# Second product of the last pair of blocks in seven products for eight, with its result turned by VectorE and stored in runs of 128 bytes

## The chip, the core and the metric

The kernel runs on one core of a Trainium2 chip. The metric is the device time in microseconds (us) of one execution, as a median over runs; the runs of one kernel lie within a few us of each other. Engines are named as the profile names them: PE is TensorE's matmul, PEld its weight load (beside PE), DVE is VectorE, ACT is ScalarE, POOL is GpSimd, SP is SyncE, which issues most DMAs; SPq and ACTq are DMA issues by SP and ACT. Each engine runs its own instructions strictly in order and waits at an instruction until what it needs is there.

## The reference, cut to what matters

A linear attention over 8 batches, 8 heads, 576 positions and head size 64 gives a matrix `x` of 4608 tokens by 512 columns. A feed-forward follows, and it is nearly all of the TensorE work:

```
h = x @ w_in          # (4608, 512) @ (512, 2048)
r = maximum(h, 0)
g = r * r
return g @ w_out      # (4608, 2048) @ (2048, 512)
```

All is float32. Each float32 operand of a matmul is split in a high and a low part, and a product is three matmuls: high by high, high by low, low by high. One part is made by a cast on ACT, the other by a subtraction on DVE or POOL.

## The kernel before, in words

The tokens are worked off in 9 blocks of 512. Blocks 0 to 2 go one by one. Blocks 3 to 8 go as three **pairs** of 1,024 tokens, called `s0`, `s1`, `s2` in the order. For a pair the first product `h` is already made with seven block products for eight (`A11 S4 S2 A12 S3 S1 A22`), for each of 8 column groups j: the weights and their sums are the stationary operand, and DVE and ACT put the products together on the two 512-token halves, the near and the far one.

The second product of a pair is made plainly. `out_unit(s, n, t)`, in the order `s1.o.n.t`, is three matmuls: 128 tokens of `g` as the stationary operand, one 128-row chunk of `w_out` (512 columns) moving. There are 32 chunks n (0 to 15 near half, 16 to 31 far half) and 4 row tiles t, so 384 matmuls for a pair. The chunks of the near half are spread through the j loop; those of the far half come behind it, as the stretch `o.16` to `o.31`. In the profile the moving operand of these matmuls is called `wp`, `wo` or `wo_back`, by where the chunk lies (a refilled ring tile, or one that was kept: of the far half `wo_back` are the chunks 17, 19, 24 and 28, `wo` 21, 26 and 30).

The `g` of the far half is made just ahead of its use. `hf` is a cast on ACT (`g<-far`), `lf` a subtraction on DVE (`g<-far,g`), two of each for a pair of chunks. Only two `g` tiles exist, each for two chunks, so `hf` and `lf` of the chunks 24 and 25 can't begin before PE is through with chunk 21, and PE needs them at chunk 24.

In the same stretch of `s1`, the operands for the first product of `s2` are made: sums `T`, their high parts (`xh_T`, ACT) and their low parts (`xl_T`, `xl_B`: DVE, some on POOL). In the order they are `x2.T*`, `x2.h*`, `x2.l*` and `x2.p*` (p is POOL).

A result is copied from PSUM (`ev`, the tile `o`, by ACT and DVE in turn) and stored in rows of 512 columns (`st`, `out_dram<-o`). SP also refills a ring of seven tiles (`refill`, `wp<-...`) with weights from DRAM.

The order of all this is a table of names written out by hand, `LIST`: the kernel emits the units in that order, and each engine gets its instructions in it. All instructions are recorded by one helper, so the profile shows them under the helper's line (L290 before, L309 after); tiles tell them apart.

Of the kernel before, what the change touches and what calls it, by code (L numbers as in the profile page):

```python
# [8 lines left out]
F32 = mybir.dt.float32  # L9
# [39 lines left out]
X_BANK, Y_BANK, Z_BANK = 1, 3, 7  # L49

# [48 lines left out]
h22_0 c0/2.1 glo21 h22_1 Lq/3.2 kx/2.3 d0/2.1 h22_2 qs/3.0 P1/2.1 h22_3 c1/2.1 o.20.0 w7.WA d1/2.1 qy/3.0 relu22
o.20.1 qm/3.1 rm22 P2/2.1 o.20.2 tb/3.0 c2/2.1 XL/2.1 xh0/2.1 o.20.3 d2/2.1 Bw/3.0 xl0/2.1 qm/3.2 h23_0 ghi22 qd/3.1  # L100
P3/2.1 glo22 h23_1 c3/2.1 qh0/2.2 h23_2 d3/2.1 Lq/3.3 w0.a1 kv/2.2 xh1/2.1 qh1/2.2 xl1/2.1 ql0/2.2 h23_3 qx/3.1
Lv/3.1 kr/2.2 o.21.0 relu23 qs/3.1 ql1/2.2 o.21.1 rm23 o.21.2 kh/2.2 qm/3.3 o.21.3 kp/2.2 B/2.3 kp/2.3 w0.s2 h24_0
ghi23 w0.s3 h24_1 glo23 h24_2 w0.s4 Lk/3.0 h24_3 kl/2.2 w0.h34 o.22.0 w0.l34 Lk/3.1 relu24 P0/2.2 o.22.1 rm24 w1.a1
o.22.2 c0/2.2 Lv/3.0 qy/3.1 w0.h12 d0/2.2 o.22.3 P1/2.2 w0.l12 ghi24 h25_0 km/3.0 c1/2.2 h25_1 h25_2 w0.W34 glo24
h25_3 d1/2.2 w0.W12 km/3.1 o.23.0 relu25 P2/2.2 XL/2.2 o.23.1 rm25 k1/3.0 o.23.2 c2/2.2 xh0/2.2 o.23.3 xl0/2.2
d2/2.2 h26_0 k2/3.0 ghi25 w1.a2 P3/2.2 h26_1 c3/2.2 glo25 qh0/2.3 h26_2 w1.s1 d3/2.2 h26_3 ql0/2.3 k1/3.1 xh1/2.2
o.24.0 relu26 o.24.1 rm26 ke/3.0 P0/2.3 o.24.2 c0/2.3 xl1/2.2 o.24.3 qh1/2.3 d0/2.3 k2/3.1 h27_0 ql1/2.3 ghi26 h27_1
kx/3.0 glo26 h27_2 w1.s2 B/3.0 P1/2.3 h27_3 ke/3.1 c1/2.3 o.25.0 relu27 d1/2.3 w1.s3 o.25.1 tb/3.1 rm27 XL/2.3 w1.s4
P2/2.3 o.25.2 c2/2.3 Bw/3.1 qd/3.2 xh0/2.3 o.25.3 d2/2.3 P3/2.3 ghi27 h28_0 xl0/2.3 Lq/4.0 c3/2.3 glo27 h28_1 kx/3.1
kz/3.0 d3/2.3 h28_2 w2.a1 xh1/2.3 kv/3.0 qh0/3.0 xl1/2.3 qx/3.2 ql0/3.0 h28_3 Lv/3.2 w1.h34 kr/3.0 o.26.0 relu28  # L110
qs/3.2 kp/3.0 o.26.1 kp/3.1 rm28 o.26.2 kh/3.0 qm/4.0 qy/3.2 o.26.3 w1.h12 Lk/3.2 h29_0 ghi28 kl/3.0 h29_1 w1.l12
glo28 Lk/3.3 P0/3.0 tb/3.2 h29_2 c0/3.0 Lv/3.3 w1.l34 h29_3 qd/3.3 P1/3.0 relu29 o.27.0 km/3.2 rm29 o.27.1 c1/3.0
o.27.2 qx/3.3 B/3.1 k1/3.2 o.27.3 h30_0 ghi29 k2/3.2 h30_1 XR/3.0 Lq/4.1 h30_2 glo29 h30_3 km/3.3 o.28.0 Bw/3.2
relu30 w1.W34 o.28.1 rm30 ke/3.2 o.28.2 qh0/3.1 w1.W12 k1/3.3 o.28.3 kx/3.2 ql0/3.1 XL/3.0 h31_0 ghi30 k2/3.3 h31_1
h31_2 B/3.2 w2.a2 glo30 P0/3.1 qs/3.3 h31_3 c0/3.1 w2.s1 o.29.0 relu31 XL/3.1 P1/3.1 ke/3.3 rm31 o.29.1 back.0
# [33 lines left out]
s0.0.m21 s0.R.9 s0.o.0.2 d0/5.0 s0.0.h1 Lq/6.0 s0.o.0.3 qx/5.2 s0.0.l1 P1/5.0 s0.1.A11 qs/5.2 s0.R.10 c1/5.0 st.2.3
d1/5.0 s0.0.S4 qy/5.2 s0.1.c1 k2/5.2 XL/5.0 P2/5.0 s0.o.1.0 s0.R.11 c2/5.0 s0.0.a12 s0.1.S2 d2/5.0 s0.0.rf0 tb/5.2  # L150
P3/5.0 s0.1.A12 s0.1.u2 k1/5.3 qd/5.3 Bw/5.2 c3/5.0 s0.o.1.1 d3/5.0 s0.R.12 qx/5.3 XR/5.0 s0.1.S3 s0.1.r11 qs/5.3
Lq/6.1 s0.1.S1 s0.1.m11 qy/5.3 s0.1.u3 qm/6.0 s0.1.h0 s0.o.1.2 s0.R.13 s0.0.qf0 s0.1.l0 s0.o.1.3 s0.1.a22 s0.1.A22
# [157 lines left out]
def attention_ffn_kernel(ctx: ExitStack, tc: tile.TileContext, q, k, v, w_in, w_out, out):  # L310
# [820 lines left out]
    X, Y, Z = (banks[i] for i in (X_BANK, Y_BANK, Z_BANK))  # L1131
    g_tiles = {}

    def g_at(s, n):
# [202 lines left out]
```

## Time and profile before

| | |
|---|---|
| median of 3 runs | 840.65 us (838.52 to 841.83) |
| profiled execution | 838.89 us |
| its span in the profile | 837.1 us |
| PE busy | 828.8 us, 99% |
| DVE busy | 540.8 us, 65% |
| ACT busy | 486.7 us, 58% |
| POOL busy | 288.2 us, 34% |

The span runs from the first to the last instruction or DMA of the profiled execution; 1.8 us of its time lie around it. Busy shares are means over stages: DVE's 65% is made of stretches in which it is nearly full and others in which it is nearly idle.

### The profile page before, as it was taken

How to read it: one execution, taken by the hardware profiler on the slowest of the kernel's cores; microseconds unless marked ns; L12 is line 12 of the kernel's file. 1: busy time of each engine (PE TensorE's matmuls, PEld its weight loads, DVE VectorE, ACT ScalarE, POOL GpSimd, SP SyncE). 2: the span in 40 equal slices, each digit the busy share in tenths (PEclk: the TensorE clock that was granted, in tenths of full speed). 3: DMA queues.
4: the chain of work that ended last, by engine and by line, in shares of the span. 5: the costliest groups of instructions: out<-in, count | busy, mean ns of one | idle time of the engine just before them, and what ended most of it. 6: DMA issues, size and time to landing. Idle time of an engine off the chain costs nothing.

```text
span 837.1 us, 12969 instructions
## 1 busy us (share of the span) xinstructions
PE 828.8 (99%) x4286; PEld 678.2 (81%) x4286; DVE 540.8 (65%) x1098; ACT 486.7 (58%) x898; POOL 288.2 (34%) x269
## 2 busy tenths in 40 slices
PE   8999999999999999999999999999999999999997
PEld 6778787888888888888888888888888888888886
DVE  7898888878787789957687887653257132222421
ACT  4888866666656656676667455566464144444411
POOL 4578654467667656242322342211004000000000
PEclk9999999999999999999999999999999999999999
DMA  9969987973688889999889857865575375554611
GB/s 240 270 186 299 279 287 214 327 215 98 211 256 249 227 283 259 277 281 258 234 252 245 283 159 213 271 187 189 172 233 177 98 227 156 163 166 154 186 55 50
DMA packets 156594, 179.65 MB, mean 215 GB/s; under 512 B 51696, under 2 KB 120304, under 8 KB 156528
## 3 DMA queue, kind: packets, MB, share of 16 engines
q1 hardware_dynamic: 155776, 177.88, 71.7%
q10 hardware_dynamic: 752, 0.95, 0.4%
q8 instruction: 34, 0.56, 0.3%
q14 instruction: 32, 0.26, 0.1%
HBM read 133.69 MB, written 45.09 MB: 214 GB/s over the span
## 4 chain that ended last, share of the span: by engine, by line
PE 90%; DVE 4%; DMA 2%; issue 1%; POOL 1%; ACT 1%; SPq 1%; DVEq 0%; POOLq 0%; ACTq 0%
PE bank L290 90%; DVE m L290 1%; DMA raw_o<-in_moe_w_out_dram 1%; DMA qt<-in_q_dram 1%; SPq L290 1%; DMA raw_i<-in_moe_w_in_dram 0%; POOL qs L290 0%; DVE qs L290 0%; DVE g_lo L290 0%; DVE w L290 0%; POOL qn L290 0%; DVE xf L290 0%; DVE bank L290 0%; DVE r L290 0%; DVE qm L290 0%
## 5 line engine op out<-in xcount | busy, mean ns | idle before, releaser
L290 PE MATMUL bank<-wp,g 128*128 128x512 f32 x648 | 160.7, 390 | 0.0
L290 PEld LDWEIGHTS bank<-wp,g 128*128 128x128 f32 x648 | 120.6, 188 | 24.9
L290 PE MATMUL bank<-x_hi,wi 128*128 128x512 f32 x384 | 131.3, 396 | 0.0
L290 PE MATMUL bank<-xh_T,wp 128*128 128x512 f32 x384 | 130.7, 390 | 0.0
L290 PE MATMUL bank<-wo,g_hi 128*128 128x512 f32 x384 | 120.3, 394 | 0.0
L290 PE MATMUL bank<-xh_B,wp 128*128 128x512 f32 x288 | 98.0, 390 | 0.0
L290 POOL TENSOR_TENSOR qs<-qT,qs 64x640 fp32r<-64x640 f32 (+1 forms) x40 | 64.2, 1604 | 94.4 <-ACT qs L290 63.1
L290 DVE TENSOR_TENSOR c<-c,bank 128x512 f32<-128x512 f32 x48 | 32.9, 686 | 86.7 <-ACT c L290 86.4
L290 PEld LDWEIGHTS bank<-xh_T,wp 128*128 128x128 f32 x384 | 72.1, 188 | 16.3 <-ACT bank L290 1.2
L290 PEld LDWEIGHTS bank<-x_hi,wi 128*128 128x128 f32 x384 | 72.2, 188 | 15.9 <-DVE x_lo L290 0.4
L290 ACT ACTIVATE far<-far 128x512 f32<-128x512 f32 x96 | 60.6, 632 | 41.1 <-DVE far L290 39.9
L290 PEld LDWEIGHTS bank<-wo,g_hi 128*128 128x128 f32 x384 | 70.5, 188 | 14.8 <-ACT g_hi L290 0.4
L290 PE MATMUL bank<-wo,g_lo 128*128 128x512 f32 x192 | 75.0, 391 | 0.0
L290 PE MATMUL bank<-x_lo,wi 128*128 128x512 f32 x192 | 74.9, 390 | 0.0
L290 PE MATMUL bank<-xl_T,wp 128*128 128x512 f32 x192 | 74.8, 389 | 0.0
L290 PE MATMUL bank<-wo_back,g 128*128 128x512 f32 x288 | 71.4, 389 | 0.0
L290 DVE TENSOR_TENSOR g<-far,g 128x512 fp32r<-128x512 f32 x48 | 35.7, 781 | 43.5 <-ACT g L290 43.4
L290 DVE TENSOR_TENSOR far<-far,bank 128x512 f32<-128x512 f32 x48 | 32.9, 685 | 47.7 <-PE bank L290 47.5
L290 PEld LDWEIGHTS bank<-xh_B,wp 128*128 128x128 f32 x288 | 54.1, 188 | 11.6
L290 PEld LDWEIGHTS bank<-wo_back,g 128*128 128x128 f32 x288 | 53.6, 188 | 11.0
L290 POOL TENSOR_TENSOR qn<-qn,qs 128x640 f32<-128x640 f32 x30 | 37.8, 1261 | 69.6 <-DVE qs L290 47.0
L290 ACT CAST g<-far 128x512 fp32r<-128x512 f32 x48 | 27.5, 619 | 49.7 <-PE bank L290 49.4
(136 smaller groups left out, 1527.0 us busy)
## 6 DMA issues: line engine op xcount, KB each, us to landing
wp<-w_outs SPq DMA_DIRECT2D x54, 512.0 KB, 4.4
wp<-w_sums SPq DMA_DIRECT2D x96, 256.0 KB, 3.8
wp<-w_own SPq DMA_DIRECT2D x72, 256.0 KB, 3.6
out_dram<-o SPq DMA_DIRECT2D x68, 128.0 KB, 2.9
raw_i<-in_moe_w_in_dram SPq DMA_DIRECT2D x16, 512.0 KB, 6.5
raw_o<-in_moe_w_out_dram SPq DMA_DIRECT2D x16, 512.0 KB, 7.1
bounce<-tb SPq DMA_DIRECT2D x24, 320.0 KB, 3.8
qT<-bounce SPq DMA_DIRECT2D x96, 80.0 KB, 2.8
```

Of the source, the lines that this page charges most:

```text
L290: ins = f(*args, **kwargs)
```

## The change

Only the last pair, `s2`, gets another second product. It is made with seven block products for eight as well: `w_out` (or sums of its quarters) becomes the stationary operand and `g` (or sums of its quarters) the moving one, 512 tokens wide. A product has 8 j by 2 column tiles d by 3 matmuls, 48 in all, and seven of them are 336 matmuls in place of 384.

- **Sums of `w_out`** (`out_sums(j)`, `t0` to `t7`, recorded in `s1`): for each j DVE makes two sums of 128x512 (`a1`, `a2`), two differences of 128x256 (`s3`, `s4`) and one low part of 128x512 (`l34`); POOL makes two differences of 128x256 (`s1`, `s2`) and one low part of 128x512 (`l12`); ACT makes two casts (`h12`, `h34`); SP stores the four halves to a new DRAM tensor `w_t`. The buffers are those of the attention, which is over by then: in the rows below they appear as `qt`, `kt`, `vt` and `sum_*`.
- **In the j loop of `s2`**: no `o` chunks; `fp.A11.j` and `fp.A12.j` (6 matmuls each) and four sums of `g` on DVE (`q.S1` to `q.S4`). The refills are those of a new list (`refill_last`), 56 tiles in place of 46.
- **Behind it**: `fp.S2`, `S1`, `S4`, `S3`, `A22`, each from casts on ACT (`fh`) and subtractions on DVE or POOL (`fl`), tile `fo`.
- **The result**: for each of C11, C12, C22, C21 and each column half d, DVE adds from PSUM (`fe`, into `o`, or into `p`, `u` on the way), turns the tile by 32x32 blocks (`ft`, `STREAM_TRANSPOSE turned<-o`), and SP or ACT stores it in runs of 32 columns (`fs`): four DMAs of 16 KB in each `fs` of C11 and C12, two of 32 KB in each of C21 and C22.

```diff
+LAST_ORDER = "A11 S2 A12 S3 S1 A22 S4".split()
+FINAL = ("S2", "S1", "S4", "S3", "A22")
+FINAL_BANKS = dict(S2=(1, 3), S1=(0, 7), S4=(2, 6), S3=(4, 5), A22=(1, 3))
...
+    def out_sums(j):
...
+        return dict(
+            a1=lambda: add(a1, 2 * j), a2=lambda: add(a2, 2 * j + 1),
+            s1=less(e.pool, s_, 0, a1, 1, a1, 0), s2=less(e.pool, s_, 1, a2, 1, s_, 0),
+            s3=less(e.dve, a2, 1, a2, 1, a1, 1), s4=less(e.dve, a2, 0, a2, 0, s_, 1),
+            h12=high(0), l12=low(0, e.pool), W12=lambda: save(0),
+            h34=high(1), l34=low(1, e.dve), W34=lambda: save(1),
+        )
...
+    def last_sum(name, j, on):
...
+        on.tensor_tensor(out, a, b, op=op)
...
+    def final_product(p, j, ds):
...
+        for d in ds:
+            f = slice(d * P, (d + 1) * P)
+            for k, (a, b) in enumerate(((0, 0), (0, 1), (1, 0))):
+                e.pe.matmul(
+                    banks[to[d]], w[:, a, f], x[:, b], start=j == 0 and k == 0, stop=j == NPR - 1 and k == 2,
+                    skip_group_check=True,
+                )
...
+    def final_out(name, d):
...
+        e.dve.tensor_tensor(out, base, bank(p), op=ALU.add)
+
+    def final_turn(name, d):
+        t = evac["t" + name, d] = w_pool.tile([P, NT], F32, name="turned", tag="w", bufs=WB)
+        e.dve.transpose(
...
+    def final_store(name, d, a, on):
...
+        for b in range(2):
...
+                on.dma_start(dst[:, :, b], src[:, :, b])
...
+fp.A22.4.1 fs.C22.1.3.a fp.A22.5.1 fs.C22.0.0.s fp.A22.6.1 fs.C22.0.2.s fp.A22.7.1 fe.C21.1 fs.C22.1.0.s ft.C21.0
+fs.C21.0.1.a fs.C21.0.0.s fs.C21.0.3.a ft.C21.1 fs.C21.0.2.s fs.C21.1.1.a fs.C21.1.0.s fs.C21.1.3.a fs.C21.1.2.s
+fs.C22.1.2.s
```

DVE before, in `s1` from the low parts for the chunks 20 and 21 to those of the last chunks; each `g<-far,g x2` is the `lf` of two chunks, the rest are operands for `s2`:

```order
L290 TENSOR_TENSOR g<-far,g 128x512 x2
L290 TENSOR_TENSOR T_6879<-xl_T_3480,xl_B_3061 128x512
L290 TENSOR_TENSOR xl_B_3061<-xl_B_3061,xh_B_3175 128x512
L290 TENSOR_TENSOR T_6891<-xl_B_3717,xl_T_3480 128x512
L290 TENSOR_TENSOR xl_T_3769<-T_6879,xh_T_3764 128x512
L290 TENSOR_TENSOR g<-far,g 128x512 x2
L290 TENSOR_TENSOR T_6921<-xl_B_3717,T_6879 128x512
L290 TENSOR_TENSOR T_6929<-xl_B_3371,T_6921 128x512
L290 TENSOR_TENSOR xl_T_3813<-T_6921,xh_T_3803 128x512
L290 TENSOR_TENSOR xl_T_3480<-T_6891,xh_T_3798 128x512
L290 TENSOR_TENSOR g<-far,g 128x512 x8
```

DVE now, from the low parts for the chunks 22 and 23 (the sixth row above) on; `qt`, `kt`, `vt` and `sum_*` hold the sums of `w_out`:

```order
L309 TENSOR_TENSOR g<-far,g 128x512 x2
L309 TENSOR_TENSOR T_6996<-xl_B_3718,T_6940 128x512
L309 TENSOR_TENSOR qt_80<-wo_957 128x512
L309 TENSOR_TENSOR T_7007<-xl_B_3372,T_6996 128x512
L309 TENSOR_TENSOR xl_T_3814<-T_6996,xh_T_3804 128x512
L309 TENSOR_TENSOR xl_T_3481<-T_6959,xh_T_3799 128x512
L309 TENSOR_TENSOR qt_80<-qt_80,kt_78 128x256
L309 TENSOR_TENSOR qt_80<-qt_80,vt_86 128x256
L309 TENSOR_TENSOR kt_79<-wp 128x512
L309 TENSOR_TENSOR qt_80<-qt_80,sum_qn 128x512
L309 TENSOR_TENSOR g<-far,g 128x512 x2
L309 TENSOR_TENSOR qt_81<-wp 128x512
```

Five instructions of the sums now stand between two pairs of low parts that had four between them, and the same goes on behind the last row, where before nothing stood between the low parts.

DVE at the very end of the program, now; `p` and `u` are partial sums, bank_89 and bank_91 hold the last product A22 for the two column halves of C21:

```order
L309 TENSOR_TENSOR o<-u_8232,bank_93 128x512
L309 TENSOR_TENSOR p_8006<-p_8006,bank_92 128x512
L309 STREAM_TRANSPOSE turned<-o 128x512
L309 TENSOR_TENSOR p_8018<-p_8018,bank_93 128x512
L309 TENSOR_TENSOR o<-p_8006,bank_89 128x512
L309 STREAM_TRANSPOSE turned<-o 128x512
L309 TENSOR_TENSOR o<-p_8018,bank_91 128x512
L309 STREAM_TRANSPOSE turned<-o 128x512 x2
```

Where two copies out of PSUM ended the program before, the add that needs the last matmul now stands ahead of the turns of both halves of C21.

SP at the very end, now, with the waits: `DMAHW` is one of eight completion counters that SP's and ACT's DMAs take in turn, `DVE` is DVE's:

```order
L309 DMA out_dram<-turned 32x8x32 [waits DMAHW1_49,DVE_49]
L309 DMA out_dram<-turned 32x8x32 [waits DMAHW3_49]
L309 DMA out_dram<-turned 32x8x32 [waits DMAHW5_49]
L309 DMA out_dram<-turned 32x8x32 [waits DMAHW7_49]
L309 DMA out_dram<-turned 32x8x32 [waits DMAHW1_49,DVE_49]
L309 DMA out_dram<-turned 32x8x32 [waits DMAHW3_49]
L309 DMA out_dram<-turned 32x8x32 [waits DMAHW4_49]
L309 DMA out_dram<-turned 32x8x32 [waits DMAHW5_49]
L309 DMA out_dram<-turned 32x8x32 [waits DMAHW6_49]
L309 DMA out_dram<-turned 32x8x32 [waits DMAHW7_49]
```

Ten stores stand behind the turn of C21's first half on SP (the first four of them its own), and ACT has eight more of the same form; each waits for the completion of the DMA that last used its counter.

## Rows read from the trace of the kernel before

**Rows 1.** The profile's page: busy us (share of the span) and instructions of each engine.

```profile
PE 828.8 (99%) x4286; PEld 678.2 (81%) x4286; DVE 540.8 (65%) x1098; ACT 486.7 (58%) x898; POOL 288.2 (34%) x269
```

**Rows 2.** The chain that ended last: start us, us, what; its end.

```profile
194.58 637.71 PE bank L290 x3178
832.28 0.02 issue
832.31 0.69 DVE o L290
```

**Rows 3.** Stretches of s1 (first two) and of one round of s2's j loop.

```profile
core 0: us, PE busy (x) PEld busy (x) DVE busy (x) ACT busy (x) POOL busy (x), PEclk, DMA share, GB/s
618.31:644.15 25.84, 25.84 (x115) 21.40 (x114) 22.06 (x31) 16.09 (x28) 7.78 (x5) 1.00 0.66 209
644.15:655.03 10.88, 10.88 (x49) 9.01 (x48) 3.77 (x5) 2.28 (x4) 2.33 (x2) 1.00 0.45 143
682.79:697.75 14.96, 14.96 (x68) 12.39 (x67) 4.13 (x7) 6.71 (x11) 0.00 (x0) 1.00 0.58 174
```

**Rows 4.** Timeline of PE: start us, us, instructions; one chunk of s1, and the end.

```profile
646.87 2.88 PE L290 MATMUL bank<-wo_back,g 128*128 128x512 f32 x12
...
826.67 2.88 PE L290 MATMUL bank<-wo,g 128*128 128x512 f32 x12
829.39 2.88 PE L290 MATMUL bank<-wp,g 128*128 128x512 f32 x12
```

**Rows 5.** Timeline of DVE from 638 us: the same, with idle time before and its releaser.

```profile
638.16 1.41 DVE L290 TENSOR_TENSOR T<-xl_B,T 128x512 f32<-128x512 f32 x2
639.53 2.39 DVE L290 TENSOR_TENSOR xl_T<-T,xh_T 128x512 fp32r<-128x512 f32 x2
642.34 2.98 DVE L290 TENSOR_TENSOR g<-far,g 128x512 fp32r<-128x512 f32 x2 [0.42 <-ACT g L290]
647.78 1.30 DVE L290 TENSOR_TENSOR g<-far,g 128x512 fp32r<-128x512 f32 x2 [2.46 <-ACT g L290]
```

**Rows 6.** Timeline of POOL in the same stretch.

```profile
639.65 1.72 POOL L290 TENSOR_TENSOR xl_B<-xl_B,xh_B 128x512 fp32r<-128x512 f32 x1 [6.39 <-DVE T L290]
641.33 1.74 POOL L290 TENSOR_TENSOR xl_T<-T,xh_T 128x512 fp32r<-128x512 f32 x1
643.04 3.43 POOL L290 TENSOR_TENSOR xl_B<-xl_B,xh_B 128x512 fp32r<-128x512 f32 x2
```

**Rows 7.** Groups of DVE by form: count | busy us, mean ns of one | idle before.

```profile
L290 DVE TENSOR_TENSOR c<-c,bank 128x512 f32<-128x512 f32 x48 | 32.9, 686 | 86.7 <-ACT c L290 86.4
...
L290 DVE STREAM_TRANSPOSE tb<-qn 128x640 f32<-128x640 f32 x24 | 20.1, 838 | 3.8 <-POOL qn L290 2.6 <-DMA out_dram<-o 1.0
...
L290 DVE TENSOR_TENSOR xr<-bank,xf 64x256 f32<-64x256 f32 x48 | 19.7, 411 | 10.7 <-ACT xf L290 10.2
...
L290 DVE TENSOR_TENSOR a<-wi 128x512 f32<-128x512 f32 x8 | 8.0, 1005 | 1.5 <-POOL a L290 1.4
```

**Rows 8.** Groups of POOL by form.

```profile
L290 POOL TENSOR_TENSOR s<-s,w_sum 128x512 fp32r<-128x512 f32 x8 | 10.4, 1295 | 6.2 <-ACT w_sum L290 6.2
...
L290 POOL TENSOR_TENSOR s<-a 128x256 f32<-128x256 f32 x8 | 6.4, 795 | 6.0 <-DVE mt L290 3.1 <-DMA w_sums<-s 2.6
```

**Rows 9.** Group of ACT by form.

```profile
L290 ACT CAST g<-far 128x512 fp32r<-128x512 f32 x48 | 27.5, 619 | 49.7 <-PE bank L290 49.4
```

**Rows 10.** Timeline of DMA issues by SP: eight stores of results in a row.

```profile
787.36 5.01 SPq L290 DMA_DIRECT2D out_dram<-o  x8
```

**Rows 11.** The page's DMA issues: xcount, KB each, median us from issue to landing.

```profile
out_dram<-o SPq DMA_DIRECT2D x68, 128.0 KB, 2.9
...
x_left<-xf SPq DMA_DIRECT2D x16, 32.0 KB, 3.4
```

**Rows 12.** One store of `x_left` (32 KB, runs of 128 bytes): issue ns, landing us.

```profile
L290 SPq DMA_DIRECT2D x_left<-xf x1: 371/371/371, 434.8 to 434.8; - x1
DMA to landing us min/median/max: 2.1/2.1/2.1
```

More of the change, by code (lines that the diff above doesn't have):

```diff
@@ L99 @@
[L99 to L103, printed above, removed]
@@ L149 @@
[L149 to L152, printed above, removed]
-tb/5.3 s0.1.rf1 ke/5.2 s0.o.2.0 s0.1.r21 B/5.1 s0.o.2.1 qd/6.0 kx/5.2 s0.1.m21 s0.o.2.2 k2/5.3 s0.1.h1 s0.o.2.3
@@ L1129, in product @@
                 )
-    X, Y, Z = (banks[i] for i in (X_BANK, Y_BANK, Z_BANK))
+    Y, Z = (banks[i] for i in (Y_BANK, Z_BANK))
+    last_c = {}
     g_tiles = {}
@@ L1141, in wide @@
         c = {}
+        X = banks[X_OTHER if s == LAST and j % 2 else X_BANK]
+        if s == LAST:
+            last_c[j] = c
         def near(i):
@@ L1193, in wide @@
         return u
+    w_t = dram.tile([NPR, 2, P, 2, 2, 2 * P], F32, name="w_t")
+    seq = [(j, p) for j in range(NPR) for p in LAST_ORDER]
+    last_tiles = []
+    for n in range(0, len(seq), 2):
+        last_tiles.append(("w", seq[n : n + 2]))
+        if n % 7 in (5, 6):
+            j = len([1 for t in last_tiles if t[0] == "b"])
+            last_tiles.append(("b", j))
+    for p in FINAL:
+        last_tiles += [("f", (p, i)) for i in range(NPR // 2)]
+    final_w, final_op, slots, evac = {}, {}, {}, {}
@@ new lines, in refill_last @@
+    def refill_last(n):
+        kind, i = last_tiles[n]
+        t = stay.tile([P, 2, 2, 2 * P], F32R, name="wp", tag=RING[(LAST * len(tiles_of) + n) % len(RING)])
+        for k in range(2):
+            if kind == "w":
+                j, name = i[k]
+                held[LAST, (j, name)] = t[:, k]
+                if name[0] == "A":
+                    src = w_own[j, :, ("A11", "A12", "A22").index(name)]
+                else:
+                    a, m = divmod(int(name[1]) - 1, 2)
+                    src = w_sums[j, a, :, :, m]
+            elif kind == "b":
+                src = w_outs[2 * i + k][:, :, : 2 * P]
+                final_w[("A11", "A12")[k], i] = t[:, k]
+            else:
+                j = 2 * i[1] + k
+                final_w[i[0], j] = t[:, k]
+                name = FINAL_OF[i[0]]
+                if name == "B22":
+                    src = w_outs[2 * j + 1][:, :, 2 * P :]
+                else:
+                    a, m = {"T1": (0, 0), "T2": (0, 1), "T4": (1, 0), "T3": (1, 1)}[name]
+                    src = w_t[j, a, :, :, m]
+            e.sp.dma_start(t[:, k].bitcast(F32), src)
@@ new lines, in spare, with buffer, add, less @@
+    def spare(n):
+        if n not in spares:
+            if n < 7:
+                t = (kt[0], kt[1], qt[0], qt[1], vt[0], vt[1], qT)[n].rearrange("p a b c -> p (a b c)")
+            else:
+                name = ("q_lo", "q_hi", "qn", "ke")[n - 7]
+                t = attn_pool.tile([P, 2 * LOW * D], F32, name="sum_" + name, tag=name)
+            spares[n] = t[:, :NT]
+        return spares[n]
+    spares = {}
+    def out_sums(j):
+        def buffer(n):
+            return spare(n).rearrange("p (c f) -> p c f", c=2)
+        i = j % 2
+        a1, a2, s_ = (lambda: buffer(i)), (lambda: buffer(2 + i)), (lambda: buffer(4 + i))
+        hi = (lambda: buffer(7 + i)), (lambda: buffer(9 + i))
+        low_of = s_, a2
+        def add(t, fc):
+            w = wo_at[fc] if fc in wo_at else wo_at[LAST - 1, fc + NFC * (j < SUMS_LATE)]
+            e.dve.tensor_tensor(
+                t().rearrange("p c f -> p (c f)"), w[:, 0].bitcast(F32), w[:, 1].bitcast(F32), op=ALU.add
+            )
+        def less(on, out, k, a, ka, b, kb):
+            return lambda: on.tensor_tensor(out()[:, k], a()[:, ka], b()[:, kb], op=ALU.subtract)
+        def high(n):
+            return lambda: e.act.copy(hi[n]().bitcast(F32R), low_of[n]())
+        def low(n, on):
+            t = low_of[n]
+            return lambda: on.tensor_tensor(t().bitcast(F32R), t(), hi[n](), op=ALU.subtract)
+        def save(n):
+            e.sp.dma_start(w_t[j, n, :, 0], hi[n]())
+            e.sp.dma_start(w_t[j, n, :, 1], low_of[n]())
+        return dict(
[5 more added lines that the diff above has]
+        )
@@ new lines, in slot @@
+    def slot(n):
+        if n not in slots:
+            if n < 11:
+                slots[n] = spare(n)
+            elif n < 17:
+                t = stay.tile([P, 2, NT], F32, name="sum", tag=f"o{KEPT[(n - 11) // 2]}")
+                slots[n], slots[n + 1] = t[:, 0], t[:, 1]
+            else:
+                t = late.tile([P, 4, NT], F32, name="sum", tag="x_hi1" if n == 17 else "x_lo1")
+                for i in range(4):
+                    slots[n + i] = t[:, i]
+        return slots[n]
@@ new lines, in last_source @@
+    def last_source(name, j):
+        c = last_c[j]
+        if name in ("S3", "A22"):
+            return c["far"][:, name == "A22"]
+        return slot(3 * j + ("S1", "S2", "S4").index(name))
+    def last_sum(name, j, on):
+        c = last_c[j]
+        out = last_source(name, j)
+        a, b, op = dict(
+            S1=(c["far"][:, 0], c["far"][:, 1], ALU.add), S2=(last_source("S1", j), c[0], ALU.subtract),
+            S3=(c[0], c["far"][:, 0], ALU.subtract), S4=(c[1], last_source("S2", j), ALU.subtract),
+        )[name]
+        on.tensor_tensor(out, a, b, op=op)
@@ new lines, in final_out, with bank, fresh @@
+    def final_out(name, d):
+        def bank(p):
+            return banks[{"A11": (2, 6), "A12": (4, 5)}.get(p, FINAL_BANKS.get(p))[d]]
+        def fresh():
+            evac[name, d] = w_pool.tile([P, NT], F32, name="o", tag="raw", bufs=RAWB)
+            return evac[name, d]
+        if name == "p1":
+            evac["p1", d] = work.tile([P, NT], F32, name="p1", tag=f"r{d}")
+            return e.act.copy(evac["p1", d], bank("A11"))
+        p1 = evac["p1", d]
+        if name == "U4":
+            evac["U4", d] = work.tile([P, NT], F32, name="u4", tag=f"g_hi{d}")
+        base, p = dict(
+            C11=("p1", "A12"), U2=("p1", "S2"), U4=("p1", "S1"), C12=("U4", "S4"),
+            C22=("U4", "S3"), U3=("p1", "S3"), C21=("p1", "A22"),
+        )[name]
+        base = evac[base, d] if name != "U4" else p1
+        out = fresh() if name[0] == "C" else evac["U4", d] if name == "U4" else p1
+        e.dve.tensor_tensor(out, base, bank(p), op=ALU.add)
@@ L1284, in run @@
             elif args[0] == "R":
-                refill(s, int(args[1]))
+                if s == LAST:
+                    refill_last(int(args[1]))
+                else:
+                    refill(s, int(args[1]))
             else:
```

386 lines of the change are left out of this document (230 added, 156 removed).

## The prediction

> **What bounds the kernel now.** I read the page first: PE is busy for 99% of the span, all other engines well below [rows 1]. Then the chain of waits: from 194.58 us on it is PE alone for 637.71 us, 3178 matmuls without one wait in it, up to the last matmul's end at 832.28; behind that stand one copy on DVE and the stores [rows 2]. So any matmul that is taken away shortens the run by its own length, as long as nothing makes PE wait, and all that is put behind the last matmul is added. The table of stretches then shows what has room beside PE, at a granted clock of 1.00 throughout [rows 3]. In the far half's chunks of s1 it is little on DVE: from chunk 14 to chunk 23 (618.31 to 644.15) it is busy for 22.06 of 25.84 us. In s2's j loop there is much: 4.13 of 14.96 us for DVE, 6.71 for ACT.
>
> **The matmuls.** Twelve matmuls start 829.39 - 826.67 = 2.72 us after the twelve before [rows 4], 0.2267 us each. 336 in place of 384 are 48 fewer: **-10.9 us**. Before, stationary and moving operands were 128x128 and 128x512 too, and weight loads lay beside the matmuls, so the size of one matmul stays as it is.
>
> **The sums of w_out, beside PE.** By the order they begin at chunk 10 of s1. In the j loop a set of them is 3 x 0.69 + 2 x 0.41 = 2.9 us of DVE, some 4 with what POOL costs it (below), beside 4 us that the loop takes in 15: room enough, 0 taken (0 to 1). From chunk 14 to 23, though, stand nine sums, four low parts (13 x 0.69 us, by c<-c,bank) and eight differences (0.41 us, by the 256-wide xr<-bank,xf) [rows 7]: 8.9 + 3.3 = 12.2 us. With 22.06 that is 34.3 us in 25.84, over by 8.5.
>
> POOL's part makes it worse. The two xl_T and the two low parts on DVE took 2.39 and 2.98 us, beside POOL's own subtractions; without a neighbour such pairs took 1.41 and 1.30 [rows 5, 6]. POOL was busy there for 1.72 + 1.74 + 3.43 = 6.89 us, and DVE lost 1.0 + 1.7 = 2.7, so 0.39 us for each us of POOL. POOL gets eight differences of 0.795 and four low parts of 1.295 in this stretch [rows 8], 11.5 us: 4.5 us more on DVE, 13.0 us over in all.
>
> Who waits for it: DVE works in order, and the low parts of the far half's g stand among the sums. Those for chunk 24 were done at 642.34 + 2.98 = 645.32 [rows 5]; PE begins that chunk at 646.87 [rows 4]. So 1.55 us of lateness are free; what is beyond makes PE wait, at the chunks 20, 22, 24, each time some us. With 13.0 over, 11.4 us reach PE; without any effect of POOL it would be 6.9; and if the new work also spread POOL's work so that the 2.7 us lost before were not lost again, 4.2. From chunk 23 to 27 five full-size and four half-size instructions of the sums (5.1 us) and some 3 us by POOL join 3.77 us of 10.88 [rows 3]: no catching up, no more loss. I take **+10 us** (4 to 18; the upper end is the third rival), nearer to 11.4 than to 6.9 because rows of this very stretch show DVE lengthened.
>
> Here a rule bears on it: the Trainium skill, "SBUF — State Buffer", section "SBUF: two separate sides", says that a DVE instruction with two SBUF inputs and a GpSimd one that reads SBUF exclude each other for a whole instruction. The trace doesn't show that fully: the two low parts ended at 645.32 while POOL was busy to 646.47 [rows 5, 6].
>
> **s2's j loop.** A round has 54 matmuls, 12.24 us, in place of 66. Beside it DVE has 4.13 + 4 x 0.69 = 6.9 us, ACT its 6.71 [rows 3, 7]. Both fit, POOL is idle: 0. Nor do the products behind the loop wait: one lasts 10.9 us and needs eight casts of 0.62 [rows 9] and about six subtractions of 0.69, and all adds and turns put together leave DVE under 9.6 us for each. The refills have seven tiles of lead and land in under 5 us before: 0.
>
> **Behind the last matmul.** Before, 837.1 - 832.28 = 4.8 us [rows 2]: a copy, a store, its landing. Now: the last add (0.69, by c<-c,bank), then the turn of C21's first half, which stands behind it by the order (838 ns for 640 columns, 0.67 for 512), so 1.4 us until the first stores of C21 can be issued [rows 7]. SP then has ten stores to issue, at 5.01 / 8 = 0.63 us each [rows 10]; the last begins at 1.4 + 9 x 0.63 = 7.1 us. Landing takes 2.9 to 3.4 us [rows 11], and a few tenths end the span: 10.5 to 11, **+6 us**. The low bound: 0.37 us for an issue and 2.1 for a landing, as the one x_left store of the same shape took in a quiet stretch [rows 12], 1.4 + 3.3 + 2.1 = 6.8, so +2. The high bound: each store waits for the one eight before it, so 18 stores are three turns of 3.4 us or more behind 1.4, and SP may come late from the stores before: 14, so +9. I stay near the rows of out_dram, since these are the same queue at the same place.
>
> On this the Trainium skill ("DMA: Bandwidth & Descriptors", section "Specifications") asks for 512 bytes or more in a run. In the rows, 32 KB in runs of 128 bytes took 3.4 us to land, 128 KB in runs of 2 KB 2.9 [rows 11]: the rule points to the upper half of that term; no run yet shows its size for 18 stores together.
>
> **Sum.** -10.9 + 10 + 6 = +5.1 us. On the profiled execution (838.89) that is 844.0, on the median of the runs (840.65), 1.8 us higher, 845.7. I forecast **845 us**.
>
> **Rivals.**
> 1. *DVE is hardly late (faster).* Place: the low parts for the chunks 20 to 28. If DVE's idle time of before chunk 14 lets the sums run ahead, or the half-size differences take far less than 0.41 us, lateness stays near the 1.55 us of slack, and PE waits 0 to 2 us. Then -10.9 + 1 + 5 = -4.9, **835.5**. It decides from some 7 us less DVE work than I count. For it: the mean share of DVE is only 65% [rows 1]. Against: 34.3 us in 25.84 without any help of POOL. Chance 0.14.
> 2. *A smaller lateness and a short tail.* 5 us of waits, and 4 behind the last matmul: -2, **838.5**. For it: the sum without POOL, and the x_left store. Chance 0.24.
> 3. *POOL blocks DVE for its whole time.* All 11.5 us of POOL count: 22.06 + 12.2 + 11.5 - 25.84 - 1.55 = 18.4 us of waits, -10.9 + 18.4 + 6 = +13.5, **854**. It is what the exclusion would do here. Against: 0.39, not 1, in the rows. Chance 0.08.
> 4. *The stores are the larger cost.* Waits of 10 us, and a tail of 14: +8, **849**. Chance 0.14.
>
> **Numbers.** My forecast (842 to 848) has 0.40. No change that the measurement of this kernel can tell is 0.5%, 4.2 us: 836.4 to 844.9. Rival 1 is nearly all of faster: 0.13. Rival 2 and the lower part of mine (845 lies on the border, so 0.12 of the 0.40) are within: 0.36. The rest is slower: 0.51. The range for 8 in 10 is **836 to 852**: it leaves out most of the first rival's lower side and of the third.
>
> **What would show it.** In the profile after: 48 matmuls fewer in s2 and rounds of 12.24 us; PE waits released by DVE (tile g) at the chunks 20, 22, 24, 26 and 28 of s1, about 10 us in sum, with DVE busy nearly without gap from about 618 us and POOL busy beside it; low parts of 1.0 to 1.7 us each there; no wait of PE in s2; 10.5 to 11 us from the last matmul to the end, filled by SP's issues. The prediction is wrong if PE's chain stays unbroken in s1 (then DVE's sums were hidden), if waits appear in s2's loop or products instead, or if the end lasts under 7 or over 14 us.

## The result and the profile after

The changed kernel takes 851.91 us (850.5 to 853.36), against 840.78 before: the ratio is 1.0136, with a 95% interval of 1.0108 to 1.0164. The forecast was 845 us. It had the direction and the two places right. The time lies just inside the range for 8 in 10 (836 to 852) and outside that of the forecast itself (842 to 848): of the change forecast from 840.65 to 845 us, 4.4 us, the run shows 11.1.

The profiled execution took 852.65 us, its span (from its first to its last instruction) is 850.8. The page: busy time of each engine.

```profile
PE 824.2 (97%) x4238; PEld 670.2 (79%) x4238; DVE 615.9 (72%) x1202; ACT 505.5 (59%) x936; POOL 327.0 (38%) x303
```

PE has 48 matmuls fewer than in [rows 1] and DVE 75 us more to do. PE was one unbroken chain before [rows 2]; now it waits. The view of waits of PE from 560 us on: who was waited for, us in all, times, longest.

```profile
PE bank L309 <- DVE g L309: 5.3, 4, 1.7
PE bank L309 <- ACT g L309: 2.6, 3, 1.8
PE bank L309 <- DVE o L309: 0.6, 1, 0.6
```

All of it lies in the far half's chunks of s1: 0.6 us at chunk 16 (for a copy out of PSUM, tile o), 3.3 at chunk 22, 1.9 at 24, 1.7 at 26 and 1.0 at 28, and none over 0.3 us at 20. The timeline of PE there, which answers to [rows 4]:

```profile
619.13 2.88 PE L309 MATMUL bank<-wo,g 128*128 128x512 f32 x12
...
648.29 6.75 PE L309 MATMUL bank<-wp,g 128*128 128x512 f32 x22 [1.51 <-DVE g L309]
655.42 0.73 PE L309 MATMUL bank<-wo_back,g 128*128 128x512 f32 x2 [0.38 <-ACT g L309]
657.63 4.06 PE L309 MATMUL bank<-wo_back,g 128*128 128x512 f32 x10 [1.48 <-DVE g L309]
...
678.81 1.52 PE L309 MATMUL bank<-wo,g 128*128 128x512 f32 x6
```

Chunk 14 starts at 619.13, which was 618.31 [rows 3]: 0.8 us were lost before. Most of it is lost at one wait of 0.3 us for POOL's qs at 463.5 us, where the order of the work is the same in both kernels, so this isn't the change's. Chunk 24 starts at 655.42 in place of 646.87, 7.7 us later than that shift explains. Chunk 30 would be six times 2.72 us behind chunk 24 in the kernel before, at 663.19; it starts at 678.81, **14.8 us** late beside the shift. The table of stretches shows the two reasons (columns as in [rows 3]).

```profile
641.40:648.00 6.60, 3.56 (x15) 2.31 (x13) 6.52 (x7) 2.80 (x5) 4.92 (x4) 1.00 0.56 197
648.00:651.40 3.40, 3.11 (x7) 2.48 (x8) 3.40 (x6) 1.34 (x3) 1.22 (x2) 0.51 0.97 354
651.40:658.20 6.80, 4.95 (x20) 3.45 (x19) 6.67 (x9) 2.15 (x4) 4.26 (x3) 0.99 0.36 108
658.20:661.60 3.40, 3.40 (x10) 2.62 (x9) 2.49 (x3) 0.62 (x1) 2.68 (x3) 0.52 1.02 314
```

DVE (third pair of numbers) is busy for 19.1 of these 20.2 us. And the granted clock (the number behind POOL's) is at 0.51 and 0.52 in two stretches of 3.4 us, the lower of TensorE's two levels (1.2 in place of 2.4 GHz); ahead of each, PE had been busy for only 3.56 of 6.60 and 4.95 of 6.80 us.

PE's waits for ACT are 2.6 us of the 8.5. ACT works in order too, and its casts of g stand there behind casts of the sums, which wait for DVE. ACT's timeline ahead of chunk 22:

```profile
644.85 0.62 ACT L309 CAST sum_ke<-qt 128x512 fp32r<-128x512 f32 x1 [1.24 <-DVE qt L309]
645.38 1.13 ACT L309 CAST g<-far 128x512 fp32r<-128x512 f32 x2
```

In s2 nothing waits. The six matmuls of one of the two products made in its loop start 12.24 us apart (three rows of PE's timeline), as the prediction worked out:

```profile
703.56 1.52 PE L309 MATMUL bank<-g,wp 128*128 128x512 f32 x6
...
715.80 1.52 PE L309 MATMUL bank<-g,wp 128*128 128x512 f32 x6
...
728.04 1.52 PE L309 MATMUL bank<-g,wp 128*128 128x512 f32 x6
```

The end, from the timelines of PE, SP, ACT and DVE:

```profile
819.61 17.39 PE L309 MATMUL bank<-fo,wp 128*128 128x512 f32 x76
822.56 26.21 SPq L309 DMA_DIRECT2D out_dram<-turned  x40
828.13 18.62 ACTq L309 DMA_DIRECT2D out_dram<-turned  x24
832.25 0.71 DVE L309 STREAM_TRANSPOSE turned<-o 128x512 f32<-128x512 f32 x1 [1.57 <-DMA out_dram<-turned]
837.16 0.71 DVE L309 STREAM_TRANSPOSE turned<-o 128x512 f32<-128x512 f32 x1 [3.04 <-DMA out_dram<-turned]
837.01 11.76 SPq L309 DMA_DIRECT2D out_dram<-turned  x22
837.91 8.84 ACTq L309 DMA_DIRECT2D out_dram<-turned  x12
842.09 0.71 DVE L309 STREAM_TRANSPOSE turned<-o 128x512 f32<-128x512 f32 x1 [3.64 <-DMA out_dram<-turned]
844.15 0.71 DVE L309 STREAM_TRANSPOSE turned<-o 128x512 f32<-128x512 f32 x1 [1.35 <-DMA out_dram<-turned]
```

The last matmul ends at 819.61 + 17.39 = 837.00, and 13.8 us follow (4.8 before). At that moment 22 stores are still to be issued on SP and 12 on ACT (the parts of their rows from 837 us on). SP issues 40 stores in a row from 822.56 on, 0.66 us each on the mean, which includes some 4 us of waits for DMAs that refill tiles, as SP's view of waits from 815 us on has it:

```profile
SPq L309 <- DMA wp<-w_t: 4.0, 3, 2.0
```

The turns wait for DMAs, since a turned tile's buffer (there are three) is free only when its stores have landed.

From chunk 30 to the last matmul it was 832.28 - 663.19 = 169.1 us, and is 837.0 - 678.81 = 158.2. So the account of the profiled spans closes: +0.8 (before chunk 14) + 14.8 (s1) - 10.9 (matmuls) + 9.0 (end) = +13.7 us, and 850.8 - 837.1 is 13.7. The medians are 11.1 us apart: the profiled execution of the kernel before lies 1.9 us under its median, that of the changed kernel 0.7 above. So the account is one of the profiled pair.

### The profile page after: what moved, and what is told of

Same layout as the page of the kernel before. It is cut to its first block, busy times and chain, and to the rows that moved or that the text cites. A ratio compares the mean times of both kernels' runs of the same rounds, so it can differ in the third digit from the quotient of the medians.

```text
span 850.8 us, 13331 instructions
## 1 busy us (share of the span) xinstructions
PE 824.2 (97%) x4238; PEld 670.2 (79%) x4238; DVE 615.9 (72%) x1202; ACT 505.5 (59%) x936; POOL 327.0 (38%) x303
## 4 chain that ended last, share of the span: by engine, by line
PE 80%; DVE 8%; DMA 5%; SPq 2%; POOL 2%; ACT 2%; issue 1%; DVEq 0%; POOLq 0%; ACTq 0%
PE bank L309 80%; DVE qt L309 2%; SPq L309 2%; DVE g L309 1%; DMA kt<-in_k_dram 1%; DMA qt<-in_q_dram 1%; DMA vt<-in_v_dram 1%; DVE xl_T L309 1%; DVE m L309 1%; DMA wp<-w_t 1%; DVE T L309 1%; DMA out_dram<-turned 1%; POOL qs L309 1%; DMA qT<-bounce 0%; DVE kt L309 0%
## 5 line engine op out<-in xcount | busy, mean ns | idle before, releaser
L309 PE MATMUL bank<-wp,g 128*128 128x512 f32 x432 | 111.1, 396 | 4.0 <-ACT g L309 1.8
L309 PEld LDWEIGHTS bank<-wp,g 128*128 128x128 f32 x432 | 81.0, 191 | 23.1 <-DVE g L309 2.4
L309 PE MATMUL bank<-xl_B,wp 128*128 128x512 f32 x144 | 56.2, 390 | 0.0
L309 POOL TENSOR_TENSOR qn<-qt,qm 128x640 f32<-128x640 f32 x30 | 40.3, 1347 | 39.2 <-DVE tb L309 21.1
L309 PE MATMUL bank<-fo,wp 128*128 128x512 f32 x240 | 54.7, 389 | 0.0
L309 ACT ACTIVATE bank<-bank 128x512 f32<-128x512 f32 x64 | 37.3, 582 | 26.7 <-PE bank L309 25.6
```

The source lines that it names most:

```text
L309: ins = f(*args, **kwargs)
```

## The experiments

The theory after the result: the sums of w_out overload DVE where they stand in s1, with POOL making it worse; and the end is long because too many stores stand in SP's queue. Rivals are named in each expectation. Runs of the kernel before on the same chips gave 839.4 to 840.5 us; the ratios are to those. Of the edits to the order of the work the diffs below show only some units; "..." stands for the rest.

**1. No sums.**

```diff
-t5.a1
...
-t4.l34
...
-                    src = w_t[j, a, :, :, m]
+                    src = w_sums[j, a, :, :, m]
```

> Leaves out all the sums of w_out (the units t0 to t7 on DVE, POOL and ACT, and their stores); the last products read other data of the same shape in their place. Theory: these sums overload DVE, the low parts of g come late, and the 14.8 us by which chunk 30 of s1 falls behind are theirs, so this runs at about 837 us (851.9 - 14.8), with no wait of PE in s1. Rival: the waits come from something else that the change moved (casts on ACT, SP's order); then 848 to 852.

Measured: 836.08 us, ratio 0.9941 (0.9924 to 0.9957), and PE has no wait from 560 us to the end. In its trace chunk 30 starts 44.88 us behind chunk 14, as in the kernel before (663.19 - 618.31). So the 14.8 us come from the sums: by the medians it is 15.8 us.

**2. The sums without POOL's operations.**

```diff
-t5.s1 t5.s2
...
-t5.l12
...
```

> Leaves out POOL's three of the eleven operations of each sum (two differences, one low part); DVE's and ACT's stay. Theory: DVE's own work alone is over by some 7 us, POOL's part of the delay is the rest: 843 to 847 us. Rival 1: POOL blocks DVE for its whole time, then DVE alone is hardly late: 838 to 841. Rival 2: POOL doesn't matter: 850 to 852.

Measured: 842.42 us, ratio 1.0026 (1.0013 to 1.0039): under the range of the theory by 0.6, above that of the first rival. Of the 15.8 us that the sums cost, 9.5 go with POOL's part; 6.3 stay, with DVE's part, ACT's casts, the stores, and the operations on POOL for s2's operands that were there before. One wait of PE over 1 us is left in s1, and the matmuls behind it are slow (4.14 us for ten that take 2.4 further on):

```profile
651.87 4.14 PE L307 MATMUL bank<-wo_back,g 128*128 128x512 f32 x10 [2.02 <-DVE g L307]
```

What POOL does to DVE is seen in DVE's groups from 618 to 674 us, first in the changed kernel, then here (count | busy, mean ns | idle before):

```profile
L309 DVE TENSOR_TENSOR xl_T<-T,xh_T 128x512 fp32r<-128x512 f32 x6 | 6.7, 1137 | 0.0
L309 DVE TENSOR_TENSOR qt<-qt,kt 128x256 f32<-128x256 f32 x6 | 4.6, 773 | 2.2 <-POOL vt L309 2.2
...
L309 DVE TENSOR_TENSOR kt<-wp 128x512 f32<-128x512 f32 x4 | 3.8, 956 | 0.0
```

```profile
L307 DVE TENSOR_TENSOR xl_T<-T,xh_T 128x512 fp32r<-128x512 f32 x6 | 5.1, 866 | 0.0
L307 DVE TENSOR_TENSOR kt<-wp 128x512 f32<-128x512 f32 x4 | 2.7, 683 | 0.0
L307 DVE TENSOR_TENSOR qt<-qt,kt 128x256 f32<-128x256 f32 x6 | 2.5, 422 | 0.1
```

The same instructions on DVE are longer by 0.27 to 0.35 us each on the mean when POOL works.

**3. POOL's operations kept, but written aside.**

```diff
+        aside = lambda: buffer(6)
...
-            s1=less(e.pool, s_, 0, a1, 1, a1, 0), s2=less(e.pool, s_, 1, a2, 1, s_, 0),
+            s1=less(e.pool, aside, 0, a1, 1, a1, 0), s2=less(e.pool, aside, 1, a2, 1, aside, 0),
...
-            h12=high(0), l12=low(0, e.pool), W12=lambda: save(0),
+            h12=high(0), W12=lambda: save(0),
+            l12=lambda: e.pool.tensor_tensor(aside().bitcast(F32R), aside(), hi[0](), op=ALU.subtract),
```

> POOL's three operations of each sum stay, with the same inputs and sizes, but write to a buffer aside that no other engine reads, so nothing waits for POOL; DVE, ACT and the stores read old data in its place. Leaving these operations out gave 9.5 us. Theory: DVE's two-input operations get longer beside POOL (some 9 us by the groups of DVE), and waits for POOL are a small part (2.2 us): most of the 9.5 us stays, 848 to 851 us. Rival: it was the waits for POOL's results in DVE's and ACT's order: 842 to 845.

Measured: 853.52 us, ratio 1.0174 (1.0147 to 1.0201), nothing gained at all, and 2.5 us above the expected range. So it is POOL's running beside DVE that costs, not the waits for its results. One caveat: DVE's waits for POOL are 2.1 us in this trace and 2.2 in the changed kernel's. In both they are waits until POOL has read what DVE is to overwrite; this run keeps them, so their share isn't tested.

**4. The turn ahead of the last add.**

```diff
-fe.C21.1 fs.C22.1.0.s ft.C21.0
+ft.C21.0 fe.C21.1 fs.C22.1.0.s
```

> Only moves the turn of C21's first half ahead of the add that waits for the last matmul. Step of the prediction: that turn stands behind the add, so this would give back up to 1.4 us (850.5). Theory now: the turns wait for a free buffer, and that for SP's queue of stores, so nothing changes: 851 to 853.

Measured: 851.05 us, ratio 1.0129 (1.0105 to 1.0153), not to be told from the changed kernel's 1.0136. The step of the prediction that put 0.7 us on this order was no part of the cost: the turn had no free buffer anyway.

**5. A quarter of the stores.**

```diff
-fs.C11.0.1.s
...
-fs.C21.1.3.a
```

> The changed kernel with a quarter of the stores of the last pair's result (24 of 96 DMAs; three of four groups of 32 columns are not written). Turns, order and queues stay. Theory: the number of stores on SP's queue is what makes the end long: behind the last matmul 1.4 us, two to four stores of 0.6 and a landing of 2, 5 to 6 us in place of 13.8, so 843 to 845 us. Rival: the landing of a store in runs of 128 bytes sets it, then it stays above 848.

Measured: 844.5 us, ratio 1.0054 (1.0037 to 1.007). Its last matmul ends at 838.5, its span at 843.7: 5.2 us in place of 13.8. By the medians that is 7.4 us gained. A quarter of the stores is a quarter of the bytes too, and this run doesn't tell the two apart. That it is the number fits the times of the issues, which don't grow with the size: four 16 KB stores in a row took 0.63 us each, the last 22 of SP, most of 32 KB, 0.53 each.

**6. Six buffers for the turned tiles.**

```diff
-        t = evac["t" + name, d] = w_pool.tile([P, NT], F32, name="turned", tag="w", bufs=WB)
+        if name == "C11":
+            t = w_pool.tile([P, NT], F32, name="turned", tag="w", bufs=WB)
+        else:
+            t = spare(("C12", "C22", "C21").index(name) * 2 + d)
+        evac["t" + name, d] = t
```

> The changed kernel with six buffers of their own for the turned tiles of C12, C22 and C21; queues and order as they are. Theory: SP's row of 40 stores at 0.65 us sets the end, and the turns wait only because those stores free their buffers late: 850.5 to 852, at most 1 us gained. Rival: three buffers are the cause, then most of what the even queues and buffers together gave (4.5 us) comes back: 847 to 849.

Measured: 852.27 us, ratio 1.0146 (1.0124 to 1.0167). No gain, as expected (the range ended at 852).

**7. Even queues, three buffers.** Half of C11's stores go to ACT, each store stands close behind its turn, and C21's first turn ahead of the last add.

```diff
-fs.C11.0.1.s
+fs.C11.0.1.a
...
-fs.C21.1.2.s fs.C22.1.2.s
+fs.C21.1.2.s
...
```

> The changed kernel with the even queues alone, the turned tiles in their three buffers as before. Theory: buffers alone gave nothing because SP's row of stores was the limit; with even queues, three buffers are a second limit, since each turn must wait for the landing of an earlier tile's stores: between the two, 848 to 850.5 us. Rival: queues are all of it: 847 to 848.

Measured: 849.95 us, ratio 1.012 (1.009 to 1.015): inside the expected range, but its interval lies over that of the changed kernel, so a gain isn't shown.

**8. Even queues and six buffers.** The two edits above together.

> The same stores, shared evenly between SP and ACT from C11 on, each issued as soon as its tile is turned, and the turned tiles of C12, C22 and C21 in six buffers of their own. Theory: the end is long (13.8 us behind the last matmul) because SP has 40 stores in a row at 0.65 us and the turns wait for buffers; with some 64 stores in two even queues the last ones start about 5 us sooner: 845 to 848 us. Rival: landing of short runs sets the end, then it stays at 850 to 853.

Measured: 847.45 us, ratio 1.0079 (1.0064 to 1.0094). From its last matmul to the end:

```profile
837.72 4.12 ACTq L308 DMA_DIRECT2D out_dram<-vt  x8
838.04 2.46 SPq L308 DMA_DIRECT2D out_dram<-qt  x5
838.31 0.69 DVE L308 TENSOR_TENSOR o<-p,bank 128x512 f32<-128x512 f32 x1 [2.78 <-PE bank L308]
839.03 0.71 DVE L308 STREAM_TRANSPOSE vt<-o 128x512 f32<-128x512 f32 x1
840.60 4.34 SPq L308 DMA_DIRECT2D out_dram<-vt  x8
```

No turn waits for a DMA, and the span ends at 847.0, 8.7 us behind the last matmul (838.31) in place of 13.8. Neither edit alone gives this. Even queues leave the turns waiting for buffers; buffers leave 40 stores on SP. The time is 4.5 us less than the changed kernel's.

**9. The sums later, first try.** Sums 7 and 0 to 4 from chunk 22 on, each behind the low parts of its pair of chunks; only adds that must read a tile before it is refilled stay early.

```diff
+SUM_BUFFERS = (
+    (3, 7, 8, 3, 9), (10, 2, 4, 10, 5), (1, 0, 8, 1, 9), (6, 3, 4, 6, 5),
+    (7, 10, 8, 7, 9), (1, 3, 5, 8, 10), (0, 2, 4, 7, 9), (6, 0, 4, 6, 5),
+)
...
-s1.o.22.0 t2.h12 t2.l12 t2.h34 t3.a1 s1.4.hf0
+s1.o.22.0 s1.4.hf0
...
+s1.o.30.2 t4.h12 t4.l12 t4.h34 s1.o.30.3
```

> The changed kernel with the sums 7 and 0 to 4 of w_out moved behind chunk 22 of s1, each behind the low parts of its pair of chunks; only the adds that must read a ring tile before it is refilled stay early. The same instructions are all there. Theory: what cost 14.8 us is the place of the sums in DVE's order, not their work, since behind chunk 23 DVE is idle for over half of the time: no wait of PE, granted clock 1.00, 836 to 840 us. Rival 1: DVE with POOL beside it is too slow there as well, 843 to 848. Rival 2: the refills come late behind the adds, PE waits for a DMA at the start of s2, 841 or more.

Measured: 852.86 us, ratio 1.0154 (1.0131 to 1.0178). A miss, but not by either rival: the wait moved. PE waits 5.2 us less for `g` (2.7 in place of 7.9), and then 9.9 us once, at the start of s2. PE's and ACT's timelines there:

```profile
671.13 0.84 PE L313 MATMUL bank<-wp,g 128*128 128x512 f32 x3
681.91 0.79 PE L313 MATMUL bank<-xh_T,wp 128*128 128x512 f32 x1 [9.93 <-ACT bank L313]
...
680.23 0.62 ACT L313 CAST sum_q_lo<-sum_q_hi 128x512 fp32r<-128x512 f32 x1 [4.72 <-DVE sum_ke L313]
680.76 0.61 ACT L313 CAST sum_qn<-sum_ke 128x512 fp32r<-128x512 f32 x1
681.28 0.58 ACT L313 COPY bank<-bank 128x512 f32<-128x512 f32 x1
```

The copy that S2 needs (the last row) stands behind two casts of the last sum, and these wait for a chain over DVE and POOL.

**10. That try with the even queues and buffers.** The edits of 8 and 9.

> The later sums and the even queues with buffers together. Theory: the two costs are in different places and add up: 851.9 - 14.5 - 4.5 = 833 us (831 to 835.5), faster than both kernels. Rival: with s1's waits gone SP's refills and stores collide at the end, 836 or more.

Measured: 848.79 us, ratio 1.0103 (1.0084 to 1.0121), far above the expected 831 to 835.5. It is 4.1 us under 9: the end is worth the same there, but the sums gave nothing yet.

**11. The sums later, second try.** They begin at chunk 24, but for six adds that must read a tile before it is refilled; casts and low parts of a set stand behind the low parts of the next pair of chunks; the last two sets lie in s2's j loop, and two more buffers are used.

```diff
+SUM_BUFFERS = (
+    (12, 1, 5, 12, 10), (3, 0, 4, 3, 9), (2, 11, 5, 2, 10), (6, 8, 4, 6, 9),
+    (12, 7, 5, 12, 10), (1, 3, 5, 8, 10), (0, 2, 4, 7, 9), (0, 11, 4, 0, 9),
+)
...
-s1.5.lf1 s1.o.25.0 t4.a2 t4.s1 t4.s2 x2.pB221
+s1.5.lf1 t7.a1 t7.s1 t7.s2 s1.o.25.0 t4.a2 x2.pB221
...
+s2.0.l0 t2.W12 t2.W34 t3.h12 t3.h34
```

> A second try at moving the sums, mended after what the first one showed: there the last set stood so late that ACT's casts for it held up the copy which the first product of s2 waits for (9.9 us). Here the sets 7 and 0 to 4 begin at chunk 24, each set's casts and low parts stand behind the low parts of the next pair of chunks, and the last two sets lie in the j loop of s2, where all their inputs are ready early; buffers are given out anew, and the work is the same. Theory: place and not work is what cost 14.8 us, so no wait of PE over 1 us and 836 to 840 us. Rival: wherever they stand, these chains over DVE, POOL and ACT hold up something that PE waits for: 843 or more.

Measured: 838.24 us, ratio 0.9983 (0.9966 to 0.9999). 13 to 14 us of the sums' cost are gone with the same instructions in another place and order, and with two more buffers. PE still waits 2.0 us for two copies of ACT at the start of s2.

**12. That with the even queues and buffers.** The edits of 8 and 11, and one more pair of stores on ACT.

> The second placing of the sums together with the even queues and own buffers of the turned tiles (one pair of stores more on ACT than there). Theory: the two costs lie in different places and add: 851.9 - 14.5 - 4.5 - 1 = 832 us (830 to 835), faster than both kernels. Rival: SP's queue at the end is worse with s1's waits gone: 836 or more.

Measured: 835.33 us, ratio 0.9938 (0.9917 to 0.996): faster than both kernels, 3 us over the expected value and just beyond its range. Its stretches, the first three at the same times as in s1 of the changed kernel, the last behind the last matmul:

```profile
618.30:641.35 23.05, 23.05 (x103) 19.12 (x102) 21.61 (x30) 16.11 (x29) 4.62 (x3) 1.00 0.87 297
641.35:655.42 14.07, 14.07 (x64) 11.66 (x63) 12.50 (x15) 3.73 (x7) 7.94 (x6) 1.00 0.40 113
655.42:672.32 16.90, 16.04 (x71) 12.96 (x71) 15.69 (x19) 7.56 (x14) 10.92 (x10) 1.00 0.66 230
...
826.80:834.70 7.90, 0.00 (x0) 0.00 (x0) 1.40 (x2) 0.00 (x0) 0.00 (x0) 0.84 0.59 92
```

The clock stays at 1.00 through s1, and 7.9 us follow the last matmul. Its span of 834.7 us is 2.4 under that of the kernel before, in place of the matmuls' 10.9. Of the difference 3.1 us are the longer end, 2.7 lie between chunk 30 and the last matmul (1.6 of them are waits), and 2.7 before chunk 14, which starts at 621.02 in place of 618.31:

```profile
621.02 2.88 PE L313 MATMUL bank<-wo,g 128*128 128x512 f32 x12
```

Of these last, 2.4 us are lost before 200 us already, where the order of the work is that of the kernel before; no run here shows why.

## Why the prediction was right in kind and too small

**Right.** The matmuls gave 10.9 us (169.1 against 158.2). A round of s2 takes 12.24 us, and nothing in s2 waits. The sums make the low parts of the far half's g late, PE waits for them at four of the five chunks named (22, 24, 26 and 28), and DVE is full there. Behind the last matmul the stores set the end.

**The step that failed first: "no catching up, no more loss" from chunk 23 to 27.** The term was +10, all of it up to chunk 23; it measured 14.8, of which 7.7 had come by the start of chunk 24 and 7.1 came behind it, where some 4.1 us are waits of PE and 1.6 matmuls at half clock. The step's own numbers were 5.1 + 3 + 3.77 = 11.9 us in 10.88, and it let that pass as even, while DVE's instructions there are again longer beside POOL. The table of the whole stretch from chunk 24 to chunk 28:

```profile
655.42:672.32 16.90, 13.39 (x49) 9.92 (x49) 14.21 (x14) 4.57 (x9) 12.52 (x11) 0.90 0.70 233
```

POOL is busy for 12.52 of these 16.9 us. From 618.3 to 672.3 POOL is busy for 29.5 us, some 18 more than in the run without its part (11.3), and five groups of DVE with two SBUF inputs, by count and mean, are 8.6 us longer (three of them are shown with experiment 2). So DVE loses some 0.5 us for each us of POOL, where 0.39 was taken. How much POOL would work was nearly right: 11.5 us up to chunk 23, and the 3 us of loss put behind it are 7.7 us of POOL at 0.39. What was wrong is the rate, and that the second part of the loss was let pass as even. The range held the time (4 to 18 us). That 6.9 us for DVE alone lies near the 6.3 of experiment 2 is partly luck: in that trace the wait of 2.0 us is for a pair of low parts that DVE made beside POOL's earlier work, and half clock follows it, neither of which the 6.9 contains.

**What had no term: the clock.** Of the 14.8 us PE's waits are 8.5. Matmuls at half clock are some 3.2 more: 22 of them from 648.29 take 6.75 us where 5.15 would be due (22 x 0.2267 and the 0.16 by which the last one outlasts the start of the next), ten from 657.63 take 4.06 for 2.43. The last 3 us are left to the eight interruptions, where matmuls no longer overlap (two take 0.73 us there); that share was not taken apart by a run.

**What had no term either: ACT's order.** The 2.6 us of PE's waits for ACT come from casts of g behind casts of the sums. The prediction followed DVE's order alone; no run takes this share apart from DVE's lateness, on which these casts wait.

**The other mis-sized term: the end, +6 against +9.0.** The prediction counted the ten stores of SP behind the turn of C21's first half and put the stores from before into a bound (+9). At the last matmul's end SP had 22 stores to go, and the turns waited for their buffers. That was the fourth rival's mechanism, at its price. Experiments 5 to 8 show it: with a quarter of the stores 8.6 of the 13.8 us go, and even queues help clearly only with buffers.

**The rivals.** POOL blocking DVE for its whole time was held unlikely because of the 0.39 in the rows, and because two low parts on DVE ended while POOL was still busy. Both read the rows too coarsely, since the blocking is by single instructions. POOL's and DVE's timelines in the changed kernel show it:

```profile
654.29 1.60 POOL L309 TENSOR_TENSOR vt<-vt,sum_q_lo 128x512 fp32r<-128x512 f32 x1 [1.36 <-DVE qt L309]
654.88 1.56 DVE L309 TENSOR_TENSOR qt<-qt,sum_qn 128x512 fp32r<-128x512 f32 x1
659.61 1.28 POOL L309 TENSOR_TENSOR xl_B<-xl_B,xh_B 128x512 fp32r<-128x512 f32 x1
659.69 1.48 DVE L309 TENSOR_TENSOR qt<-qt,kt 128x256 f32<-128x256 f32 x1 [0.91 <-POOL vt L309]
```

POOL's first ends at 655.89, DVE's at 656.44, 0.55 us later; the second pair ends at 660.89 and 661.17, 0.28 us apart. From 618.3 to 674 us each of the 21 instructions of DVE with two inputs in SBUF that began while one of POOL ran ended 0.55 to 0.60 us (128x512) or 0.28 us (128x256) behind it, however long it had run; unhindered they take 0.68 and 0.41 us. Rows 5 and 6 show the same before the change: the xl_T pair ended at 639.53 + 2.39 = 641.92, 0.55 us behind POOL's 639.65 + 1.72 = 641.37. So this case's traces agree with the whole-instruction lock of the Trainium skill ("SBUF — State Buffer", section "SBUF: two separate sides"). POOL in its turn waits for DVE, and its busy time includes that; so the loss is 0.5 us for each busy us of POOL on the mean, and not 1. The third rival had the mechanism right and its price too high: 18.4 us of waits, where s1 cost 14.8. That the time of 851.91 lies near its 854 is luck, since the end made up for it.

The second rival (5 us of waits, 4 behind the last matmul) fell with 14.8 and 13.8. That DVE is hardly late, the first, fell with experiment 1.

The Trainium skill ("DMA: Bandwidth & Descriptors", section "Specifications") asks for 512 bytes or more in a run. What runs of 128 bytes cost in landing no run here shows, since none stores the same bytes in long runs. The 34 stores issued behind the last matmul, of 16 and 32 KB, landed as the view of DMAs has it:

```profile
DMA to landing us min/median/max: 1.5/1.8/2.0
```

The sum that would have come out right for the profiled pair is -10.9 + 14.8 + 9.0 + 0.8.

## What to carry to other kernels

Look at the stretch and not at the mean: DVE had 85% of this one filled already, and 12.2 us of new work met 3.8 us of free time there, though its mean share was low. Look for a stretch that is empty, and follow each chain through every in-order queue before moving it: the first try at moving the sums only handed the wait from DVE's queue to ACT's. Price a store in many small DMAs by the queue's whole backlog at the last matmul, not by the stores of the last tile, and count its buffers too. A wait of PE can cost more than its length: here 8.5 us of waits came with 14.8 us of delay.

## What the runs showed of the hardware that was not expected

- With waits of 0.4 to 1.8 us among its matmuls, TensorE was granted half clock in two stretches of the profiled execution (0.51 from 648.0 to 651.4 and 0.52 from 658.2 to 661.6 us); with the waits gone (experiment 12) the clock stayed at 1.00 through s1.
- An instruction of DVE with two inputs in SBUF that began while one of POOL ran ended 0.55 to 0.60 us (128x512) or 0.28 us (128x256) behind it. The same holds where nobody reads what POOL writes (21 of 21 in experiment 3). On the mean DVE lost some 0.5 us for each busy us of POOL.
- POOL's instructions get longer too: a 128x512 low part took 1.5 us on the mean of six beside a busy DVE (1.61 in the row), where the same form took 1.295 before [rows 8].

```profile
662.74 1.61 POOL L309 TENSOR_TENSOR vt<-vt,sum_q_hi 128x512 fp32r<-128x512 f32 x1 [0.43 <-DVE qt L309]
```
